# Expert weights: a longer way from load to split, other staging room, and scatters without an order among themselves

## The chip, the cores and the metric

The kernel runs on one core of a Trainium2 chip. The time is the device time of one execution in microseconds (us), less is better. The engines are TensorE (PE in the profile, with its weight loads as PEld), VectorE (DVE), ScalarE (ACT), GpSimd (POOL) and SyncE (SP), which here only issues DMA transfers. Each engine works through its own queue strictly in order; semaphores order the queues among each other.

## What is computed

Attention with global and local keys and a bias by distance feeds a dense layer with the activation h - tanh(h), and that feeds a layer of eight experts of which each token takes one. The reference, cut to its core:

```
x = attention(q, k, v)            # 3072 tokens x 512
h = x @ w_in                      # 512 x 2048, the dense layer
x = (h - np.tanh(h)) @ w_out
logits = x @ w_gate               # the layer of experts
e_idx = np.argmax(logits, axis=1)
gate_w = softmax(logits)[e_idx];  eom = sigmoid(x @ w_output_gate)
for e in range(8):
    mask = e_idx == e
    h = np.maximum(x[mask] @ w1[e], 0.0)          # 512 x 1024
    out[mask] = gate_w[mask] * eom[mask, e] * (h @ w2[e])
```

Every product is made of three matmuls in a reduced 32-bit float: each operand is split into a high part (a cast) and a low part (the operand minus its high part), and high x high, high x low and low x high are added up in PSUM.

## The kernel before

The 3072 tokens go through in 12 blocks of 256. A list of numbered sub-steps (`at(gt, rank, fn)`, 32 per block) says in which order the program is written; from that a scheduler, which works with a timeline of its own, makes the order of the instructions in each engine's queue. Position in the list is therefore a wish, and the queues are the fact.

The dense layer (`moe_h`, `moe_y`) takes 16 slices u of 128 columns of w_in in each block: 12 matmuls `ph`, on ACT and DVE the activation (`uu`, `tt`, `ss`, `vt`, `gg`), its high part `gh` on ACT and its low part `gl` (on DVE in block 0, on POOL in the others), and then 6 matmuls `y`: four with `gh`, two with `gl`.

After a block comes the routing: the rows of y go to `yrow` (`rt_evac`), are transposed (`yT`), the logits come out of `lp` and `lg`, the rank of each token within its expert out of `rk`, and from it DVE makes the row address `su`. Two scatters on POOL, 128 rows each, then write the rows to the sorted buffer `srt` in DRAM (`scatter`). `cnt_c` counts the tokens of each expert.

The experts work in jobs. Expert 0, the one with the most tokens, has two: job 0 takes its first 256 rows, which are known once block 10 has been scattered, and job 1 the other 256, which need block 11 as well. Jobs 2 to 8 are the experts 1 to 7. A job loads its rows (`xr`, on SP's queue), transposes them on PE (`xTp`), splits them (`xTh` on ACT, `xTl` on DVE), and then goes through 8 steps f: 12 matmuls `h2p`, the split with Relu (`h2h` on ACT, `h2l` on DVE), and 6 to 12 matmuls `ob`. At its end the results go to `orow` and are scattered to the output.

The weights of an expert come in eight pieces of 512 KB: 0 to 3 of w1 and 4 to 7 of w2. `ex_load` issues the load on SP into a staging tile `ex`, `ex_split` makes the high part `eh` on ACT and the low part `el` on DVE. All staging tiles are of the tag "row" of three buffers, which `yrow` and the `orow` of job 0 take as well. In the list, piece f of the next expert is loaded in step f of a job and piece f - 1 is split in it.

Of the kernel before, what the change touches and what calls it, by code (L numbers as in the profile page):

```python
# [9 lines left out]
F32 = mybir.dt.float32  # L10
# [22 lines left out]
def kernel(  # L33
# [15 lines left out]
    nc = tc.nc  # L49
    P = 128  # L50
# [3 lines left out]
    E, _, F = w1.shape  # L54
    TB = 256
    NBLK = NT // TB
# [13 lines left out]
    NF2 = F // P  # L70
# [9 lines left out]
    srt = dram.tile([E * RS, W], F32, name="srt")  # L80
# [3 lines left out]
    def w8(name, dt=F32R):  # L84
        t = persist.tile([P, 2048], dt, tag="w8", bufs=16, name=name)
        return t

    def rowt(name):
        t = persist.tile([P, 1024], F32, tag="row", bufs=3, name=name)
        return t  # L90

    def bank(tag, bufs, name):
        t = psum.tile([P, 512], F32, tag=tag, bufs=bufs, name=name)
        return t
# [35 lines left out]
    agenda = {}  # L130

    def at(gt, rank, fn):
        agenda.setdefault((gt, rank), []).append(fn)

    def run(gt):
        for rank in range(-2, 5):
            fns = agenda.setdefault((gt, rank), [])
            while fns:
                if rank == -2:
                    with tc.high_priority():  # L140
                        fns.pop(0)()
                else:
                    fns.pop(0)()
# [453 lines left out]
    def moe_h(blk, u, gt):  # L597
        fg, fo = divmod(u, 4)
        ph = bank("h", 2, f"ph{blk}_{u}")
        n = 0  # L600
        for kc in range(KC):
            o = kc * 512 + fo * P
            whi, wlo = wih[fg][:, o : o + P], wil[fg][:, o : o + P]
            for lw, xx in ((whi, xhi), (whi, xlo), (wlo, xhi)):
                nc.tensor.matmul(ph[:, 0:TB], lw, xx[blk][:, kc, :], start=(n == 0), stop=(n == 3 * KC - 1))  # L605
                n += 1

        def tmp(tag, bufs, dt=F32):
            t = p1.tile([P, TB], dt, tag=tag, bufs=bufs, name=f"{tag}{blk}_{u}")
            return t  # L610

        L = {}

        def gate():
            hps = ph[:, 0:TB]
            uu = L["uu"] = tmp("uu", 2)
            ss = L["ss"] = tmp("ss", 2)
            tt = L["tt"] = tmp("tt", 2)
            vv = L["vv"] = tmp("vt", 2)
            nc.scalar.activation(uu, hps, AF.Square)  # L620
            nc.scalar.activation(tt, hps, AF.Tanh)  # L621
            nc.scalar.activation(ss, uu, AF.Square, scale=G_S, bias=ga[:, 0:1])  # L622
            nc.vector.scalar_tensor_tensor(out=vv, in0=uu, scalar=G_C, in1=hps, op0=ALU.add, op1=ALU.mult)  # L623
            nc.vector.tensor_tensor(out=tt, in0=tt, in1=hps, op=ALU.subtract)  # L624
            nc.vector.scalar_tensor_tensor(out=vv, in0=ss, scalar=G_S2B, in1=vv, op0=ALU.add, op1=ALU.mult)

        def gate2():
            uu, ss, tt, vv = L["uu"], L["ss"], L["tt"], L["vv"]
            gg = L["gg"] = tmp("gg", 2)
            if blk < 1:  # L630
                nc.scalar.activation(ss, uu, AF.Relu, bias=nt2[:, 0:1])
            else:
                nc.vector.tensor_scalar(out=ss, in0=uu, scalar1=G_T2, scalar2=None, op0=ALU.is_gt)
            nc.vector.tensor_tensor(out=gg, in0=vv, in1=uu, op=ALU.mult)  # L634
            nc.vector.copy_predicated(gg, ss.bitcast(I32), tt)  # L635

        def parts():
            gg = L["gg"]
            gh = tmp("gh", 3, F32R)
            gl = tmp("gl", 3, F32R)  # L640
            nc.scalar.copy(gh, gg)  # L641
            by = nc.vector if blk < 1 else nc.gpsimd
            by.tensor_tensor(out=gl, in0=gg, in1=gh.bitcast(F32), op=ALU.subtract)  # L643
            g_t[blk, u] = (gh, gl)

        at(gt + 1, 0, gate)
        at(gt + 2, 0, gate2)
        at(gt + 3, 0, parts)

    def moe_y(blk, u):  # L650
# [14 lines left out]


    rts = {}
    last_rows = []

    def rt_evac(blk):  # L670
        for j in range(2):
# [24 lines left out]
    def rt_logits(blk, gt):  # L696
# [92 lines left out]
        def scatter(j):  # L789
            r = rts.pop((blk, "row", j))  # L790
            store = nc.gpsimd.indirect_dma_start(
                out=srt[:, :], out_offset=IndirectOffsetOnAxis(ap=L["su"][:, j : j + 1], axis=0),
                in_=r[:, 0:W], in_offset=None, bounds_check=E * RS - 1, oob_is_err=False,
            )
            if blk == NBLK - 1:
                last_rows.append(store.ins)
                if j == 1:
                    tc.declare_no_dep(last_rows[1], last_rows[0], reason="each token has one row")

        last = blk == NBLK - 1  # L800
        rk = -2 if last else 0
# [4 lines left out]
        at(gt + 3, rk, step4)  # L806
        at(gt + 3, rk, step5)
        at(gt + 4, rk, lambda: scatter(0))
        at(gt + (4 if last else 6), rk, lambda: scatter(1))

    def plan_route(blk, gt):
# [50 lines left out]
    def expert(r):  # L862

        if r not in ordering:
            ordering[r] = nc.values_load(
                order_i[0:1, r : r + 1], engines=[mybir.EngineType.SP], min_val=0, max_val=E - 1
            )
        return ordering[r]
# [4 lines left out]
    NP = 8  # L873

    def ex_load(e, i):
        st = rowt(f"ex{e}_{i}")
        rv = expert(e)
        if i < 4:
            nc.sync.dma_start(st, w1[ds(rv, 1), i * P : (i + 1) * P, :].rearrange("o p f -> p (o f)"))
        else:  # L880
            r = (i - 4) * 2 * P
            nc.sync.dma_start(
                st.rearrange("p (c d) -> p c d", c=2),
                w2[ds(rv, 1), r : r + 2 * P, :].rearrange("o (c p) d -> p (o c) d", p=P),
            )
        staged["e", e, i] = st

    def ex_split(e, i):
        hd, ld = (w1h, w1l) if i < 4 else (w2h, w2l)
        t = (i % 4) // 2  # L890
        if i % 2 == 0:
            hd[e, t] = w8(f"eh{e}_{i}")
            ld[e, t] = w8(f"el{e}_{i}")
        st = staged.pop(("e", e, i))
        sl = slice((i % 2) * 1024, (i % 2 + 1) * 1024)
        hi = hd[e, t][:, sl]
        nc.scalar.copy(hi, st)  # L897
        nc.vector.tensor_tensor(out=ld[e, t][:, sl], in0=st, in1=hi.bitcast(F32), op=ALU.subtract)  # L898
# [17 lines left out]
    def ex_rows(n):  # L916
        r, j0, _ = jobs[n]
        rv = expert(r)
        for j, m in tiles(n):
            t = job_tile(n, "xr", [P, W], F32, f"xr{n}_{j}")  # L920
            nc.sync.dma_start(t[0:m, :], srt[ds(rv * RS + (j0 + j) * P, m), :])
            xrows[n, j] = t
# [5 lines left out]
    def n_groups(n):  # L928
        return KC // 2 if jobs[n][2] == 256 else KC
# [238 lines left out]
    for blk in range(NBLK):  # L1168
        G = 32 * blk
        for u in range(NF):  # L1170
            g = G + 2 * u
# [7 lines left out]
    G = 32 * (NBLK - 1)  # L1179
    at(G - 32 + 20, 2, order_experts)  # L1180
    for i in range(NP):
        at(G + 10 + 2 * i, 0, lambda i=i: ex_load(0, i))
        at(G + 12 + 2 * i, 0, lambda i=i: ex_split(0, i))

    pools.update({
# [14 lines left out]
    for i in range(4):  # L1200
        at(G + 1 + 2 * steps[i], 4, lambda i=i: ex_load(1, i))
        at(G + 5 + 2 * steps[i], 4, lambda i=i: ex_split(1, i))
    for gt in range(min(g for g, _ in agenda), G - 32 + 24):
        run(gt)

    pa.release()
    p2a = ctx.enter_context(tc.tile_pool(name="p2a", bufs=1, side="right", reuse_waits="tile"))
    for k in range(3):
        pools["xr", k] = p2a, "xr", 4
    for nm in ("xTh", "xTl"):  # L1210
        pools[nm, 1] = p2a, "xTa", 4
    for gt in range(G - 32 + 24, 32 * NBLK + 32):
        run(gt)


# [32 lines left out]
    for n in range(1, len(jobs)):  # L1248
        e = jobs[n][0]
        for f in range(NF2):  # L1250
            ex_s1(n, f)
            if n == 1:
                for i in range(NP):
                    if steps[i] - NF2 == f:
                        ex_load(1, i)
                    if steps[i] + 2 - NF2 == f and i >= 4:
                        ex_split(1, i)
            elif e + 1 < E:
                ex_load(e + 1, f)
                if f >= 1:  # L1260
                    ex_split(e + 1, f - 1)
            if f >= 1:
                if n < len(jobs) - 1 or f - 1 < NF2 - LATE:
                    ex_s2(n, f - 1)
            elif n > 1:
                ex_s2(n - 1, NF2 - 1)
                ex_out(n - 1)
            if n + 1 < len(jobs):
                if f == 2:
                    ex_rows(n + 1)  # L1270
                if 4 <= f < 4 + n_groups(n + 1):
                    ex_T(n + 1, f - 4)
                if f == NF2 - 1 and n > 1:
                    ex_split(e + 1, NP - 1)

    n = len(jobs) - 1
    with tc.manual_schedule(engines={mybir.EngineType.PE}):
# [134 lines left out]
```

## Time and profile before

| what | value |
|---|---|
| median of 3 runs | 1174.91 us (1173.6 to 1175.56) |
| the profiled execution | 1180.22 us |
| its span in the trace | 1178.4 us |
| PE busy in the span | 1114.1 us, 95% |
| DVE, ACT, POOL busy | 854.4, 672.6, 215.1 us |

The profile is of one execution, 5.3 us above the median. A busy time counts an instruction from its start to its end; matmuls overlap each other, so their spacing is shorter than their duration (a matmul of 256 columns lasts 0.28 us and follows the one before it by 0.12 us).

### The profile page before, as it was taken

To read this page: it belongs to the slowest core of one execution; us is meant where nothing else is said; L and a number is where in the kernel's file an instruction comes from. 1 tells how busy PE (TensorE), PEld (TensorE's weight loads), DVE (VectorE), ACT (ScalarE), POOL (GpSimd) and SP (SyncE) were. 2 spreads that over 40 slices of the span, in tenths; PEclk is the share of its full clock that TensorE was granted. 3 is DMA by queue.
4 is the path that set the end of the run, shared out by engine and by line. 5 is a ranking of instruction groups with operands and counts; after the bars stand their busy time and mean duration, and the time that the engine had idled before them with its cause. 6 is when DMAs were issued, how large, how long until landed. Compare 5 with 4: busy or idle time off the path is not lost.

```text
span 1178.4 us, 22198 instructions
## 1 busy us (share of the span) xinstructions
PE 1114.1 (95%) x7374; PEld 948.8 (81%) x7374; DVE 854.4 (73%) x2704; ACT 672.6 (57%) x1794; POOL 215.1 (18%) x281
## 2 busy tenths in 40 slices
PE   3798899999999999999999999998999999999995
PEld 1476688888888888888888888887888778888894
DVE  4869978889989889989889888998463434434410
ACT  3989876666666666666666667565352333434310
POOL 1000012222222222222222222323100110110100
PEclk9799899999999999999999999999999999999998
DMA  6733492111211112121102121123471633625200
GB/s 177 237 105 122 143 275 53 28 48 33 55 38 39 37 39 51 30 55 30 49 21 55 37 55 26 38 72 110 136 260 59 204 97 107 206 91 163 78 23 24
DMA packets 128850, 103.25 MB, mean 88 GB/s; under 512 B 101679, under 2 KB 101679, under 8 KB 128720
## 3 DMA queue, kind: packets, MB, share of 16 engines
q1 hardware_dynamic: 124592, 89.06, 26.7%
q0 software_dynamic: 4128, 12.61, 2.8%
q8 instruction: 62, 1.02, 0.4%
q14 instruction: 68, 0.56, 0.2%
HBM read 90.04 MB, written 21.88 MB: 95 GB/s over the span
## 4 chain that ended last, share of the span: by engine, by line
PE 74%; DVE 7%; ACT 7%; DMA 5%; issue 5%; POOL 1%; SPq 1%; POOLq 0%; DVEq 0%; ACTq 0%
PE y L660 21%; PE ph L605 19%; PE ob L998 11%; PE h2p L971 9%; PE sc L495 3%; PE xp L558 3%; DMA ex<-in_moe_w_dram 3%; PE pt L544 2%; ACT pr L520 1%; PE wlo L268 1%; PE pk L431 1%; PE xTp L939 1%; PE yT L687 1%; DVE el L898 1%; DVE gg L634 1%
## 5 line engine op out<-in xcount | busy, mean ns | idle before, releaser
L643 POOL TENSOR_TENSOR gl<-gg,gh 128x256 fp32r<-128x256 f32 x176 | 148.3, 843 | 454.9 <-ACT gh L641 360.6
L605 PE MATMUL ph<-xhi,wh 128*128 128x256 f32 x768 | 219.1, 288 | 3.3 <-DVE tt L624 2.7
L605 PE MATMUL ph<-xhi,wl 128*128 128x256 f32 x768 | 218.6, 286 | 0.4 <-DVE wl L264 0.4
L605 PE MATMUL ph<-xlo,wh 128*128 128x256 f32 x768 | 217.2, 283 | 0.0
L660 PE MATMUL y<-wh,gh 128*128 128x512 f32 x384 | 158.7, 413 | 2.6 <-ACT gh L641 2.5
L605 PEld LDWEIGHTS ph<-xhi,wh 128*128 128x128 f32 x768 | 144.6, 189 | 16.6 <-DVE tt L624 5.3
L660 PE MATMUL y<-wl,gh 128*128 128x512 f32 x384 | 154.7, 403 | 0.0
L605 PEld LDWEIGHTS ph<-xlo,wh 128*128 128x128 f32 x768 | 145.0, 189 | 7.8 <-issue 0.3
L605 PEld LDWEIGHTS ph<-xhi,wl 128*128 128x128 f32 x768 | 144.8, 189 | 5.8 <-issue 3.7
L660 PE MATMUL y<-wh,gl 128*128 128x512 f32 x384 | 140.2, 411 | 2.5 <-POOL gl L643 2.5
L641 ACT CAST gh<-gg 128x256 fp32r<-128x256 f32 x192 | 78.8, 410 | 88.2 <-DVE gg L635 70.6
L976 DVE SCALAR_TENSOR_TENSOR h2l<-h2p,h2h 128x448 fp32r<-128x448 f32 (+3 forms) x72 | 40.0, 558 | 105.8 <-ACT h2h L975 105.8
L620 ACT ACTIVATE uu<-ph 128x256 f32<-128x256 f32 x192 | 74.0, 386 | 73.1 <-PE ph L605 65.8
L898 DVE TENSOR_TENSOR el<-ex,eh 128x1024 fp32r<-128x1024 f32 x64 | 77.7, 1223 | 50.2 <-ACT eh L897 49.4
L520 ACT ACTIVATE pr<-pr,sst 128x256 f32<-128x256 f32 (+1 forms) x192 | 93.5, 491 | 34.5 <-DVE sst L512 34.5
L623 DVE SCALAR_TENSOR_TENSOR vt<-uu,ph 128x256 f32<-128x256 f32 x192 | 79.9, 416 | 45.3 <-ACT tt L621 43.9
L975 ACT ACTIVATE h2h<-h2p 128x448 fp32r<-128x448 f32 (+3 forms) x72 | 35.4, 494 | 128.5 <-PE h2p L971 127.7
L897 ACT CAST eh<-ex 128x1024 fp32r<-128x1024 f32 x64 | 66.6, 1051 | 63.1 <-DMA ex<-in_moe_w_dram 48.0
L998 PE MATMUL ob<-eh,h2h 128*128 128x512 f32 x232 | 93.4, 403 | 7.4 <-ACT h2h L975 7.3
L622 ACT ACTIVATE ss<-uu,ga 128x256 f32<-128x256 f32 x192 | 99.5, 519 | 0.0
L971 PE MATMUL h2p<-xTh,eh 128*128 128x448 f32 (+3 forms) x288 | 98.0, 343 | 0.0
L971 PE MATMUL h2p<-xTl,eh 128*128 128x448 f32 (+3 forms) x288 | 97.6, 340 | 0.0
(199 smaller groups left out, 2521.7 us busy)
## 6 DMA issues: line engine op xcount, KB each, us to landing
ex<-in_moe_w_dram SPq DMA_DIRECT2D x64, 512.0 KB
vv<-vg SPq DMA_DIRECT2D x92, 96.0 KB
srt<-zrow SPq DMA_DIRECT2D x32, 257.0 KB
m<-in_moe_w_in_dram SPq DMA_DIRECT2D x16, 512.0 KB
m<-in_moe_w_out_dram SPq DMA_DIRECT2D x16, 512.0 KB
xr<-srt SPq DMA_DIRECT2D x25, 257.0 KB
qk<-in_q_dram SPq DMA_DIRECT2D x92, 64.0 KB
qk<-in_k_dram SPq DMA_DIRECT2D x92, 64.0 KB
```

The lines of the kernel that those rows point to most:

```text
L520: nc.scalar.activation(pr[j][:, c0:], pr[j][:, c0:], AF.Exp, bias=st[:, j : j + 1], scale=-1.0, accum_out=st[:, 2 + j : 3 + j],)
L605: nc.tensor.matmul(ph[:, 0:TB], lw, xx[blk][:, kc, :], start=(n == 0), stop=(n == 3 * KC - 1))
L620: nc.scalar.activation(uu, hps, AF.Square)
L622: nc.scalar.activation(ss, uu, AF.Square, scale=G_S, bias=ga[:, 0:1])
L623: nc.vector.scalar_tensor_tensor(out=vv, in0=uu, scalar=G_C, in1=hps, op0=ALU.add, op1=ALU.mult)
L641: nc.scalar.copy(gh, gg)
L643: by.tensor_tensor(out=gl, in0=gg, in1=gh.bitcast(F32), op=ALU.subtract)
L660: nc.tensor.matmul(yb[blk, j], gx[:, j * P : (j + 1) * P], wx[fg][:, sl], start=(u == 0 and n == 0), stop=(u == NF - 1 and n == 2),)
L897: nc.scalar.copy(hi, st)
L898: nc.vector.tensor_tensor(out=ld[e, t][:, sl], in0=st, in1=hi.bitcast(F32), op=ALU.subtract)
L971: nc.tensor.matmul(ph[:, 0:N], lw, xx, start=(i == 0), stop=(i == 3 * KC - 1))
L998: nc.tensor.matmul(ob[n, j][0:m, :], gx[:, j * P : j * P + m], wx, start=(f == 0 and i == 0), stop=(f == NF2 - 1 and i == 2),)
```

## The change

Four things are changed. Piece f - 2 instead of f - 1 is split in step f of a job, and the last two pieces in the first two steps of the next. The pieces of expert 0 and the first four of expert 1 are staged in tiles of the tag "xTa", four buffers, in which the odd jobs keep their transposed rows; for that the attention's room is given back 28 sub-steps earlier, and the loads of expert 0 are written 4 to 12 sub-steps earlier. The scatters to `srt` are declared free of each other in all blocks (before: only the two of the last block). And `gl` of the last block is made on DVE instead of POOL.

```diff
-            by = nc.vector if blk < 1 else nc.gpsimd
+            by = nc.vector if blk in (0, NBLK - 1) else nc.gpsimd
...
-            if blk == NBLK - 1:
-                last_rows.append(store.ins)
-                if j == 1:
-                    tc.declare_no_dep(last_rows[1], last_rows[0], reason="each token has one row")
+
+            tc.declare_no_dep(store.ins, group="srt", reason="each token has one row")
+            tc.add_to_no_dep_group("srt", store.ins)
...
     def ex_load(e, i):
-        st = rowt(f"ex{e}_{i}")
+        if e == 0 or (e == 1 and i < 4):
+
+            st = p2a.tile([P, 1024], F32, tag="xTa", bufs=4, name=f"ex{e}_{i}")
+        else:
+            st = rowt(f"ex{e}_{i}")
...
-        at(G + 10 + 2 * i, 0, lambda i=i: ex_load(0, i))
+        at(G + max(2 * i - 2, 2 * i + 4 if i >= 4 else 0), 0, lambda i=i: ex_load(0, i))
         at(G + 12 + 2 * i, 0, lambda i=i: ex_split(0, i))
...
-    for gt in range(min(g for g, _ in agenda), G - 32 + 24):
+    for gt in range(min(g for g, _ in agenda), G - 32 - 4):
...
-            elif e + 1 < E:
-                ex_load(e + 1, f)
-                if f >= 1:
-                    ex_split(e + 1, f - 1)
+            else:
+                if f < 2 and e > 1:
+                    ex_split(e, NP - 2 + f)
+                if e + 1 < E:
+                    ex_load(e + 1, f)
+                    if f >= 2:
+                        ex_split(e + 1, f - 2)
...
-                if f == NF2 - 1 and n > 1:
-                    ex_split(e + 1, NP - 1)
```

What this does to the queues is seen at three places. In the listings a name such as `h2p0_7` is that of job 0, step 7, `rk11` is of block 11, `ex1_4` is piece 4 of expert 1, and the last number only tells tiles apart; "..." marks rows left out.

PE, from the ranks of block 11 to the transposes of job 1, before:

```order
L761 MATMUL rk11_13491<-ohb11_13480,ones_bf_69 128x8
...
L971 MATMUL h2p0_5_13547<-xTh0_0_13239,eh0_0_12810 128x256
...
L830 MATMUL cnt_c_13649<-cnt_b_76,ones_bf_69 128x8
...
L971 MATMUL h2p0_7_13597<-xTh0_0_13239,eh0_0_12810 128x256
...
L998 MATMUL ob0_0_13395<-eh0_6_13131,h2h0_6_13587 128x512
...
L939 MATMUL xTp1_0_13673<-ident_66,xr1_0_13669 128x128
L939 MATMUL xTp1_1_13682<-ident_66,xr1_0_13669 128x128
...
L998 MATMUL ob0_0_13395<-eh0_6_13131,h2h0_7_13610 128x512
```

and now:

```order
L760 MATMUL rk11_13491<-ohb11_13480,ones_bf_69 128x8
L973 MATMUL h2p0_7_13597<-xTh0_0_13239,eh0_2_12931 128x256
...
L1000 MATMUL ob0_0_13395<-eh0_6_13133,h2h0_6_13587 128x512
...
L828 MATMUL cnt_c_13649<-cnt_b_76,ones_bf_69 128x8
L1000 MATMUL ob0_0_13395<-eh0_6_13133,h2h0_7_13610 128x512
...
L941 MATMUL xTp1_0_13673<-ident_66,xr1_0_13669 128x128
L941 MATMUL xTp1_1_13682<-ident_66,xr1_0_13669 128x128
```

The ranks have moved from step 4 of job 0 into the middle of `h2p0_7`: six `h2p` and twelve `ob` matmuls remain between them and the transposes, and the last six `ob` have moved ahead of these. Ahead of this place job 0's `h2p0_0` and `h2p0_1` begin before the last `y` products instead of after them.

ACT, at the start of job 1, before:

```order
L952 CAST xTh1_0_13678<-xTp1_0_13673 128x512
L952 CAST xTh1_0_13678<-xTp1_1_13682 128x512
L1011 ACTIVATE orow0_0_13634<-ob0_0_13395,so0_13270 128x512
L975 ACTIVATE h2h1_0_13708<-h2p1_0_13695 128x256
L897 CAST eh1_4_13756<-ex1_4_13712 128x1024
L975 ACTIVATE h2h1_1_13727<-h2p1_1_13714 128x256
```

and now:

```order
L1013 ACTIVATE orow0_0_13634<-ob0_0_13395,so0_13270 128x512
L954 CAST xTh1_0_13678<-xTp1_0_13673 128x512
L899 CAST eh1_4_13756<-ex1_4_13712 128x1024
L954 CAST xTh1_0_13678<-xTp1_1_13682 128x512
L899 CAST eh1_4_13756<-ex1_5_13760 128x1024
L977 ACTIVATE h2h1_0_13708<-h2p1_0_13695 128x256
L977 ACTIVATE h2h1_1_13727<-h2p1_1_13714 128x256
```

The cast of weight piece 4 has moved between the two casts of job 1's transposed rows, and that of piece 5 ahead of `h2h1_0`.

ACT, at the change from job 2 to job 3 (expert 1 to expert 2), as it now is; before, the same rows stand there in the same order:

```order
L977 ACTIVATE h2h2_7_14242<-h2p2_7_14229 128x480
...
L1013 ACTIVATE orow2_0_14324<-ob2_0_14009,so2_13935 128x512
L1013 ACTIVATE orow2_2_14334<-ob2_2_14011,so2_13935 128x512
L899 CAST eh3_2_14476<-ex3_3_14441 128x1024
L977 ACTIVATE h2h3_0_14292<-h2p3_0_14279 128x448
```

Nothing has moved here: the cast of piece 3 still stands ahead of `h2h3_0`.

## Rows read from the trace of the kernel before

**Rows 1.** The page, part 1: engine, busy us, share, instructions.
```profile
PE 1114.1 (95%) x7374; PEld 948.8 (81%) x7374; DVE 854.4 (73%) x2704; ACT 672.6 (57%) x1794; POOL 215.1 (18%) x281
```

**Rows 2.** Stages: from:to, length, busy us of PE, PEld, DVE, ACT, POOL, clock, DMA.
```profile
190.00:755.00 565.00, 560.78 (x4357) 495.79 (x4354) 506.46 (x1813) 368.01 (x1119) 146.30 (x186) 1.00 0.16 41
755.00:810.00 55.00, 54.10 (x366) 46.72 (x364) 51.57 (x147) 35.39 (x88) 18.50 (x19) 1.00 0.22 73
810.00:818.00 8.00, 5.97 (x17) 3.99 (x16) 5.89 (x10) 2.92 (x7) 5.12 (x6) 0.79 0.42 138
...
917.00:925.00 8.00, 6.21 (x30) 4.98 (x28) 2.32 (x7) 2.96 (x5) 3.87 (x4) 1.00 0.96 289
...
1053.00:1062.00 9.00, 6.75 (x39) 5.80 (x38) 3.57 (x7) 4.09 (x6) 3.84 (x4) 1.00 0.93 314
1062.00:1091.00 29.00, 29.00 (x139) 25.96 (x140) 13.91 (x21) 12.09 (x19) 0.00 (x0) 0.94 0.50 156
```

**Rows 3.** Waits of PE, 795 to 1178 us: total us, times, longest.
```profile
PE ob L998 <- ACT h2h L975: 7.3, 4, 2.2
PE y L660 <- POOL gl L643: 2.5, 2, 1.8
PE xTp L939 <- DMA xr<-srt: 1.2, 3, 0.6
```

**Rows 4.** The chain that ended last, 915 to 930 us: start, us, what.
```profile
914.99 0.12 PE xTp L939
...
917.30 6.10 DMA ex<-in_moe_w_dram
...
923.42 0.02 ACT eh L897
...
924.38 0.55 ACT h2h L975
```

**Rows 5.** Waits of POOL over the whole span: total us, times, longest.
```profile
POOL srt L791 <- DMA srt<-yrow,su: 24.0, 9, 3.2
```

**Rows 6.** Groups by line: PE in 812.5 to 817.4, then in 800 to 812 us.
```profile
L660 PE MATMUL y<-wl,gh 128*128 128x512 f32 x3 | 1.9, 628 | 0.0
L660 PE MATMUL y<-wh,gl 128*128 128x512 f32 x4 | 1.8, 538 | 1.8 <-POOL gl L643 1.8
...
L660 PE MATMUL y<-wl,gh 128*128 128x512 f32 x8 | 3.2, 395 | 0.0
```

**Rows 7.** gl and ss by line; DVE's ss in 755 to 830; timeline at 771.
```profile
L643 DVE TENSOR_TENSOR gl<-gg,gh x16: 405/422/427, 73.4 to 155.1; 128x256 fp32r<-128x256 f32 x16
...
L633 DVE TENSOR_SCALAR ss<-uu x176: 270/294/1266, 155.8 to 812.7; 128x256 f32<-128x256 f32 x176
...
L633 DVE TENSOR_SCALAR ss<-uu 128x256 f32<-128x256 f32 x19 | 8.8, 465 | 0.4
...
771.38 0.74 POOL L643 TENSOR_TENSOR gl<-gg,gh 128x256 fp32r<-128x256 f32 x1 [1.87 <-ACT gh L641]
771.48 0.80 DVE L633 TENSOR_SCALAR ss<-uu 128x256 f32<-128x256 f32 x1
```

**Rows 8.** Timeline of PE, 834 to 847 us: start, duration, instruction, wait before it.
```profile
834.61 0.18 PE L761 MATMUL rk<-ohb,ones_bf 128*128 128x8 bf16 x1
...
845.03 0.41 PE L939 MATMUL xTp<-ident,xr 128*128 128x128 f32 x2 [0.37 <-DMA xr<-srt]
845.63 0.87 PE L939 MATMUL xTp<-ident,xr 128*128 128x128 f32 x6 [0.19 <-DMA xr<-srt]
```

**Rows 9.** The chain that ended last, 834 to 850 us.
```profile
838.48 3.72 DMA srt<-yrow,su
...
842.76 2.83 DMA xr<-srt
...
846.51 1.41 PE ob L998 x6
847.91 2.15 PE h2p L971 x18
```

**Rows 10.** The page, part 5: the weight casts on ACT.
```profile
L897 ACT CAST eh<-ex 128x1024 fp32r<-128x1024 f32 x64 | 66.6, 1051 | 63.1 <-DMA ex<-in_moe_w_dram 48.0
```

More of the change, by code (lines that the diff above doesn't have):

```diff
@@ L667 @@
     rts = {}
-    last_rows = []
     def rt_evac(blk):
@@ L1211 @@
         pools[nm, 1] = p2a, "xTa", 4
-    for gt in range(G - 32 + 24, 32 * NBLK + 32):
+    for gt in range(G - 32 - 4, 32 * NBLK + 32):
         run(gt)
```

## Prediction

> **What bounds the kernel now.** The page comes first: of the span, TensorE (PE) is busy 95% [rows 1]. The end is therefore set by how many microseconds PE waits and by the stretches in which its clock is at the lower of its two levels (1.2 instead of 2.4 GHz). Next the table by stages, to see where PE is not full [rows 2]. In the 565 us of the middle blocks it is idle 4.2 us, so there is nothing to win there. The idle time sits in the passage from the dense layer to the experts (0.9 us in 755 to 810, 2.0 us in 810 to 818, where the mean clock falls to 0.79) and in short stretches at the changes of experts (1.8 us in 917 to 925, 2.25 us in 1053 to 1062, with 0.94 of the clock in the 29 us behind it). Third, who made PE wait after 795 us: ScalarE's `h2h` (7.3 us in four waits, all at changes of experts), GpSimd's `gl` (2.5 us in two, both in the last block) and the row loads `xr` (1.2 us in three) [rows 3]. Fourth, the chain at a change of experts [rows 4]: the row loads of the next job wait in SyncE's (SP's) queue for the transposes `xTp`, the weight piece stands behind them, needs 6.10 us, and ScalarE (ACT) waits for it in a cast `eh` with `h2h`, which PE needs, queued behind.
>
> **Part 1, the split two sub-steps after its load.** The stall to be removed is the cast of `ex3_3` ahead of `h2h3_0`. The queues, not the Python loop, decide this. From the row of `h2h2_6` on, ACT's queue is row for row that of before (the third listing), and so are VectorE's (DVE's), PE's and SP's from there. The four waits stay: **0**, where their full removal would be -7.3 us [rows 3] and some -1.7 us of slow clock (0.06 of 29 us [rows 2]), -9.0.
>
> **Part 2, the scatters.** In blocks 0 to 10 GpSimd (POOL) waited 24.0 us for the first scatter's landing, nine times [rows 5]. What stood behind it is `gl`, and PE waited for `gl` only in the last block, so nine blocks give **0** (at most the 4.2 us of idle time of the middle blocks, which have other releasers). The two scatters of block 11 were free of each other before. What changes is block 10: the second scatter no longer waits, and the first job's rows come earlier.
>
> **Part 3, the last dense block: `gl` to DVE, expert 0's weights early.** To win: the 2.5 us of waits for `gl`, and the slow clock behind the longer one, where 11 `y` matmuls took 538 to 628 ns in the mean of their group, instead of about 395 [rows 6], some 2 us: -4.5. To lose: DVE takes 16 `gl` of 422 ns [rows 7], 6.8 us, and in 755 to 810 it was busy 51.6 of 55 us [rows 2], so 3.4 are free. It gets part of that back: `ss`, one of its own operations, has a median of 294 ns but a mean of 465 over the 19 instructions of 755 to 830 us, 3.3 us in all, and a long one (0.80 us) stands right beside a `gl` on POOL [rows 7]. The Trainium skill says that DVE and GpSimd take one shared port pair of SBUF as an exclusive lock and that the later one blocks (SBUF — State Buffer, section "SBUF: two separate sides"); by that rule the move is nearly free and this part alone would be worth its whole -4.5 us. The trace agrees as far as 294 against 465 ns go. Against it stands the queue: the split pieces now come in clusters, four `el` in a row around `gg_6`, so `gl` and `gg` of the neighbouring steps run late and PE meets them after `ph_7`, `ph_10` and `ph_12`. And expert 1's first four pieces are no longer held by row room, so SP issues them right behind the first job's rows, and ACT has `eh1_0` ahead of `xTh0_0` and three more casts ahead of `gh_15`. These are 4 x 512 + 2 x 257 KB, 2.6 MB, 8.2 us at the highest rate in the table (314 GB/s [rows 2]), while PE has some 5 us of work left; an estimate of 2 to 4 us of waits. I take **0** between -4.5 and +5.
>
> **Part 4, the rows of job 1.** This is the term that decides. Job 1 takes rows that block 11 scatters. From the last `rk` (834.79) to the first `xTp` of job 1 (845.03) the chain took 10.2 us [rows 8]: the addresses `su` on DVE, POOL, the scatter's 3.72, SP, the row load's 2.83 [rows 9]. Before, PE had work all that time and waited only 0.37 + 0.19 us. The change starts job 0 ahead of the last `y` products, so `y_15`, the logits and `rk` of block 11 slide back through job 0 (first listing). Behind the last `rk` there now stand 6 matmuls of `h2p` and 12 of `ob` before `xTp1_0`: 6 x 0.119 + 2 x 1.41 [rows 9] = 3.5 us. Exposed: 10.2 - 3.5 = 6.7, less the 0.56 that was waited before: **+6.1**. One `h2l` less inside the DVE steps may shorten it by 0.6 (bounds 5.5 and 6.7). The Trainium skill gives a DMA about 2.0 us of fixed cost besides its bytes (DMA: Bandwidth & Descriptors, section "Anatomy of one DMA — SWDGE (gpsimd) path"). An estimate with 2.0 us for each of the two transfers makes the chain 7.7 us and the wait 3.6 instead of 6.1.
>
> **Part 5, the start of job 1.** (a) The last six `ob`, which stood behind the transposes and covered their casts, now stand ahead: PE waits for the first cast and subtraction, **+1.0** (0.5 to 1.4, the 1.41 us of cover). (b) In ACT's queue the cast `eh1_4` now stands between the two casts of job 1's transposed rows (second listing), and its piece is issued behind the late row loads. It may take 6.10 us [rows 4] where the rows take 2.83 [rows 9]: issued 0.6 us later, it lands up to 3.9 us after them, and the cast itself is 1.05 [rows 10]. Against that PE has 14 matmuls of 0.119, 1.7 us. The subtraction `el1_4` blocks DVE in the same way. **+2** (0 to 4).
>
> **Part 6, the clock.** After waits of about 2 us it fell in two places and not in a third [rows 2]: 0.21 of 8 us, 0.06 of 29 us, and 0. After 6 us of waiting I expect a fall: **+1.5** (0 to 3.4, two such falls).
>
> **The sum.** 0 + 0 + 0 + 6.1 + 1.0 + 2 + 1.5 = 10.6 us. The profiled execution took 1180.2 us (its span is 1178.4), so one of the changed kernel would take about 1190.8. The median of the timed runs is 1174.9, 5.3 us lower; with the same difference it goes to **1185.5 us**, 0.9% slower. With all low bounds it is +1.5 (1176.4), with all high ones +20.5 (1195.4).
>
> **Rivals.** *The waits at the changes of experts go.* For it: the loop now asks for one sub-step more between load and split. Against it: the unchanged rows in all queues. Price -9.0: 1176.5 with my other terms, and it makes the kernel faster as soon as these come to less than 6.7 us, which their low bounds allow. *The last block gains all it can*: part 3 at -4.5, hence 1181. For it the long `ss` beside `gl`; against it DVE's 51.6 of 55 us. (It is what the lock rule of the Trainium skill, SBUF — State Buffer, would bring.) *ACT's queue costs more than I think*: part 3 at +5, part 5 and the clock at their high ends, hence 1193 to 1195; for it that ACT, like PE, takes its queue strictly in order behind loads of up to 6.10 us. *The change does little*: every term comes out at its low bound, and 1176 to 1177 results; against it the 3.72 and 2.83 us of this very chain.
>
> **How the numbers follow.** Two measurements of this kernel differ by about 0.2%, 2.35 us, without a change. Forecast with the gain of the last block inside it, 1177.3 to 1193: 0.68, of which 0.13 belong to the gain of the last block. Above 1193: 0.07. Within 0.2%: 0.10, half of it the first rival with my other terms. Faster: 0.15, the first rival with low other terms, and what I have not seen. So slower 0.75, same 0.10, faster 0.15. The range reaches down into the cases of no change, 1175 to 1193; forecast alone 1177.3 to 1193.
>
> **What would show it.** Part 4: PE waits 5 to 7 us at `xTp` <- DMA `xr`, right after `cnt_c` and the last `ob` of job 0, and `rk` of block 11 comes only some 3.5 us of PE work ahead of it. Part 5: ACT waits for DMA `ex` in `eh` right after that, and PE for `xTh` or `xTl`. Part 1: still about 7 us in four waits `ob` <- `h2h`. Part 3: no `y` <- POOL `gl`, but waits `y` <- `gh`, and `ss` near 0.29 us in the last block. Part 6: a lower granted clock in the stage of job 1. The prediction is wrong if the wait at `xTp` is under 3 us, if the four waits at the changes of experts are gone, or if the last block wins more than 5 us.

## The result, and the profile after

The changed kernel takes 1182.5 us (median of 4 runs, 1181.83 to 1185.3), the kernel before 1174.26 in the same comparison (4 runs, 1172.44 to 1175.56). The ratio is 1.0072, 95% interval 1.0054 to 1.0089: 8.2 us between the medians, where 10.6 were forecast (1185.5). The profiled execution has a span of 1180.1 us. The first part of its page answers to [rows 1]:

```profile
PE 1110.6 (94%) x7374; PEld 945.4 (80%) x7374; DVE 848.5 (72%) x2720; ACT 670.6 (57%) x1794; POOL 198.3 (17%) x265
```

PE has the same number of instructions and almost the same busy time; the loss is idle time, and slow clock inside busy time. Who made PE wait from 755 to 1182 us (us in total, times, longest), beside [rows 3]:

```profile
PE xTp L941 <- DMA xr<-srt: 7.6, 5, 5.7
PE ob L1000 <- ACT h2h L977: 4.7, 3, 1.9
PE h2p L973 <- ACT xTh L954: 2.2, 2, 1.6
PE y L660 <- ACT gh L641: 2.1, 4, 0.8
PE ob L1000 <- ACT eh L899: 1.5, 1, 1.5
PE y L660 <- DVE gl L643: 0.3, 1, 0.3
```

The first row has grown from 1.2 us in three: one wait alone is 5.7 us, for the row loads. The waits for `gl` on POOL are gone, and those at the changes of experts (`h2h`, `eh`) are still there. PE's timeline at the long wait, from the last rank of block 11, beside [rows 8]:

```profile
840.62 0.17 PE L760 MATMUL rk<-ohb,ones_bf 128*128 128x8 bf16 x1
...
842.85 0.18 PE L828 MATMUL cnt_c<-cnt_b,ones_bf 128*128 128x8 bf16 x1
...
850.25 0.66 PE L941 MATMUL xTp<-ident,xr 128*128 128x128 f32 x2 [5.72 <-DMA xr<-srt]
851.36 1.54 PE L941 MATMUL xTp<-ident,xr 128*128 128x128 f32 x6 [0.45 <-DMA xr<-srt]
...
856.45 0.51 PE L973 MATMUL h2p<-xTh,eh 128*128 128x256 f32 x2 [0.60 <-ACT xTh L954]
857.37 0.44 PE L941 MATMUL xTp<-ident,xr 128*128 128x128 f32 x2 [0.41 <-DMA xr<-srt]
```

From the end of the last `rk` (840.79) to the first transpose 9.46 us pass, where before 10.2 passed [rows 8]. The chain did not grow; the PE work beside it shrank to 3.7 us. What PE was waiting for shows in the chain of work that ended last (start, us, what), beside [rows 9]:

```profile
841.46 0.18 DVE su L784
...
842.49 0.34 POOL srt L790
...
843.86 3.31 DMA srt<-yrow,su
...
848.57 6.27 DMA ex<-in_moe_w_dram
854.86 1.06 ACT eh L899
...
855.95 1.23 DVE el L900
857.17 0.20 DVE xTl L955
```

Behind the scatter (3.31 us) the chain goes on through weight piece 4, its cast and its subtraction, because these stand in ACT's and DVE's queues ahead of the second half of job 1's rows. The stages (as [rows 2]) show the clock behind the wait:

```profile
190.00:755.00 565.00, 560.80 (x4358) 495.93 (x4357) 502.55 (x1813) 368.46 (x1122) 144.33 (x185) 1.00 0.16 40
...
810.00:818.00 8.00, 5.24 (x27) 3.74 (x28) 6.28 (x19) 4.83 (x9) 0.00 (x0) 1.00 0.80 293
845.00:850.00 5.00, 0.00 (x0) 0.00 (x0) 0.75 (x1) 0.07 (x1) 1.95 (x2) 0.85 0.64 209
850.00:856.00 6.00, 5.11 (x20) 3.92 (x20) 1.18 (x6) 1.72 (x3) 0.00 (x0) 0.56 1.02 352
856.00:862.00 6.00, 5.12 (x34) 4.43 (x35) 4.47 (x14) 3.57 (x6) 0.00 (x0) 1.00 0.91 284
```

In the middle blocks nothing changed (560.80 us of 565 busy, before 560.78). In 810 to 818 us, the last dense block, the clock is full now (before 0.79), but PE is busy for less of it (5.24 us, before 5.97). After the wait the granted clock is 0.56 in the mean for 6 us, mostly the lower of its two levels, and then full again.

Profiled executions lie some us apart at the start and the end (block 10's first `yT` came between 765.3 and 771.2 us in the 14 profiles of this study, with no clear order by the parts). So I measure a **passage** inside each profile: from block 10's first `yT` on PE to the first `orow` of job 2 on ACT. Both ends in the changed kernel:

```profile
766.91 0.60 PE L686 MATMUL yT<-ident,yrow 128*128 128x128 f32 x4
...
926.25 0.69 ACT L1013 ACTIVATE orow<-ob,so 128x512 f32<-128x512 f32 x1 [2.19 <-PE ob L1000]
```

That is 159.3 us. In the second profile of the kernel before (last but one of the experiments) it is 148.7, in the first 148.9. The change costs 10.4 to 10.7 us there; from this `orow` to the first one of job 6 both kernels take the same, 176.9 and 177.05 (second profile of before).

### The profile page after: what moved, and what is told of

Its sections match the earlier page's. It is cut to its first block, busy times and chain, and to the rows that moved or that the text cites. A ratio compares the mean times of both kernels' runs of the same rounds, so it can differ in the third digit from the quotient of the medians.

```text
span 1180.1 us, 22184 instructions
## 1 busy us (share of the span) xinstructions
PE 1110.6 (94%) x7374; PEld 945.4 (80%) x7374; DVE 848.5 (72%) x2720; ACT 670.6 (57%) x1794; POOL 198.3 (17%) x265
## 4 chain that ended last, share of the span: by engine, by line
PE 78%; ACT 6%; DMA 5%; DVE 5%; issue 4%; SPq 1%; POOL 0%; POOLq 0%; ACTq 0%; DVEq 0%
PE y L660 21%; PE ph L605 20%; PE ob L1000 11%; PE h2p L973 10%; PE sc L495 4%; PE xp L558 4%; DMA ex<-in_moe_w_dram 3%; PE pt L544 3%; PE wlo L268 1%; PE pk L431 1%; DVE el L900 1%; ACT pr L520 1%; PE yT L686 1%; PE xTp L941 1%; PE pq L428 1%
## 5 line engine op out<-in xcount | busy, mean ns | idle before, releaser
L643 POOL TENSOR_TENSOR gl<-gg,gh 128x256 fp32r<-128x256 f32 x160 | 131.4, 821 | 450.9 <-ACT gh L641 347.7
L973 PE MATMUL h2p<-xTh,el 128*128 128x448 f32 (+3 forms) x288 | 97.6, 340 | 0.0
```

What stands on the lines that cost most here:

```text
L973: nc.tensor.matmul(ph[:, 0:N], lw, xx, start=(i == 0), stop=(i == 3 * KC - 1))
```

## The experiments

**Theory A:** the loss is the chain of block 11's rows, exposed by as much as PE lacks work behind the last `rk`, and the start of job 1 behind it. **Theory B:** the early weights or the busier DVE slow the last block by themselves. **Theory C:** the difference is one of single executions.

In this section edit 1 is the later split, edit 2 the free scatters, edit 3 `gl` on DVE, and edit 4 the staging tiles with the earlier loads. The Parts of the prediction are cut otherwise: its Part 3 holds edits 3 and 4, and its Part 4 is the wait that follows.

Edit 1 needed no run. Built alone on the kernel before, or taken out of the changed one, it leaves all five queues as they were, row for row: the list of sub-steps is written otherwise, and the scheduler makes the same program of it.

**The other edits, one at a time, and the change without edit 3.**

```diff
 p3_only, on the kernel before
-            by = nc.vector if blk < 1 else nc.gpsimd
+            by = nc.vector if blk in (0, NBLK - 1) else nc.gpsimd
 p4_only, on the kernel before
-        st = rowt(f"ex{e}_{i}")
+        if e == 0 or (e == 1 and i < 4):
+            st = p2a.tile([P, 1024], F32, tag="xTa", bufs=4, name=f"ex{e}_{i}")
+        else:
+            st = rowt(f"ex{e}_{i}")
...
-        at(G + 10 + 2 * i, 0, lambda i=i: ex_load(0, i))
+        at(G + max(2 * i - 2, 2 * i + 4 if i >= 4 else 0), 0, lambda i=i: ex_load(0, i))
...
-    for gt in range(min(g for g, _ in agenda), G - 32 + 24):
+    for gt in range(min(g for g, _ in agenda), G - 32 - 4):
 p2_only, on the kernel before
+            tc.declare_no_dep(store.ins, group="srt", reason="each token has one row")
+            tc.add_to_no_dep_group("srt", store.ins)
 no_p3, on the changed kernel
-            by = nc.vector if blk in (0, NBLK - 1) else nc.gpsimd
+            by = nc.vector if blk < 1 else nc.gpsimd
```

> The kernel before with only the gl of the last block on DVE. In the queues this alone puts job 0's first two h2p ahead of the last y, the last rk back, and leaves 11 ob (11 x 0.235 = 2.6 us) between the last rk and the first xTp of job 1. Theory A (the chain from rk over scatter and row load is exposed by as much as PE lacks work behind the last rk): PE waits 6.5 to 7.5 us at the first xTp <- DMA xr, the waits for gl go (-2.5), clock and start of job 1 cost 1 to 3 more, so slower by 5 to 9 us, 1179 to 1183. Theory B (the loss of the change comes from the weights being staged early, which fills ACT's queue and the DMA): this run is equal to before or 2 to 4 us faster, 1170 to 1174, no wait over 2 us at xTp. Theory C (the difference is that of single executions): within 2.4 us of before.

> The kernel before with only the staging of experts 0 and 1 in xTa tiles, their earlier loads and the earlier release of the attention's room. Between the last rk and the first xTp of job 1 there are 24 h2p and 18 ob (24 x 0.119 + 18 x 0.235 = 7.1 us). Theory A: PE waits 2 to 3.5 us at the first xTp, and the start of job 1 costs up to 1 more, so slower by 1.5 to 5 us, 1176 to 1179. Theory B: the whole loss, 7 to 9 us, 1181 to 1183. Theory C: within 2.4 us of before.

> The kernel before with only the scatters to srt free of each other in all blocks. Between the last rk and the first xTp of job 1 there are 22 h2p and 18 ob (22 x 0.119 + 18 x 0.235 = 6.8 us). Theory A: PE waits 2 to 3.5 us at the first xTp, and the start of job 1 costs up to 1 more, so slower by 1.5 to 5 us, 1176 to 1179; no gain in the blocks 1 to 9, where PE stays idle 4 us in 565. Theories B and C: within 2.4 us of before.

> The changed kernel with gl of the last block back on POOL; the other three parts stay. Between the last rk and the first xTp of job 1 there are the 36 h2p and 23 ob of before (36 x 0.119 + 23 x 0.235 = 9.7 us). Theory A: the wait at the first xTp is under 1 us, and the time is that of before, 1172 to 1177, with some 2 us of waits for gl. Theory B: the loss stays, 1180 to 1184. Theory C: within 2.4 us of before as well, but then p3_only is too.

**A slice more or less of `gl` on DVE, and the chain taken away.**

```diff
 mix8, on the changed kernel
-            by = nc.vector if blk in (0, NBLK - 1) else nc.gpsimd
+            by = nc.vector if blk < 1 or (blk == NBLK - 1 and u < 8) else nc.gpsimd
 no_chain, on the changed kernel (srt_b: 256 rows, filled once with zeros)
-            nc.sync.dma_start(t[0:m, :], srt[ds(rv * RS + (j0 + j) * P, m), :])
+            if n == 1:
+                nc.sync.dma_start(t[0:m, :], srt_b[j * P : j * P + m, :])
+            else:
+                nc.sync.dma_start(t[0:m, :], srt[ds(rv * RS + (j0 + j) * P, m), :])
```

> The changed kernel with gl on DVE in the first 8 of the last block's 16 slices, on POOL in the other 8. Between the last rk and the first xTp of job 1 there are 24 h2p and 21 ob (24 x 0.119 + 21 x 0.235 = 7.8 us). Theory A: the wait at xTp1 is about 9.5 - 7.8 = 1.7 us (1 to 2.5), the waits for gl and gh in the last block about 2, so 1174 to 1178, between before and p2_only. Theory B: half the loss of the change, 1177 to 1179, with the wait at xTp1 still near 5.

> The changed kernel, gl on DVE and all, but job 1 loads its 256 rows from a second buffer that is filled with zeros at the start (two loads more there); the real rows of job 1 are left out of the result. PE's queue is the same up to the last rk and behind the transposes of job 1, which now stand right behind cnt_c, and the cast of weight piece 4 of expert 1 no longer stands between the two casts of job 1's rows. Theory A (the loss is the wait for block 11's rows and what follows from it): no wait over 1 us at xTp1, no fall of the clock behind it, 1172 to 1176, the time of before. Theory B (gl on DVE slows the last block by itself, the wait only hides it): at most half of the 8 us comes back, 1178 to 1182.

Measured, in the order of the PE work that stands between the last `rk` and the first `xTp` of job 1 (the work as in the expectations; the time from `rk` to `xTp` and the wait from each profile's timeline of PE; each ratio is to the runs of the kernel before that were timed beside that kernel, whose median was 1174.26 for the change, 1173.55 for mix8 and no_chain, 1173.1 for the others):

| kernel | PE work behind `rk`, us | `rk` to `xTp`, us | first wait at `xTp`, us | passage, us | median, us | ratio to before (95%) |
|---|---|---|---|---|---|---|
| before (two profiles) | 9.7 | 10.2, 9.7 | 0.4, 0 | 148.9, 148.7 | 1173.1 | 1 |
| no_p3 | 9.7 | 9.7 | 0 | 150.5 | 1173.03 | 1.0005 (0.9987 to 1.0022) |
| mix8 | 7.8 | 9.1 | 1.15 | 150.2 | 1173.65 | 0.9992 (0.9976 to 1.0008) |
| p4_only | 7.1 | 8.7 | 1.47 | 154.1 | 1176.42 | 1.0016 (0.9998 to 1.0033) |
| p2_only | 6.8 | 10.0 | 3.02 | 152.9 | 1177.82 | 1.0037 (1.0019 to 1.0055) |
| the change | 3.5 | 9.5 | 5.72 | 159.3 | 1182.5 | 1.0072 (1.0054 to 1.0089) |
| p3_only | 2.6 | 9.5 | 6.70 | 163.3 | 1186.17 | 1.0092 (1.0068 to 1.0116) |
| no_chain | none needed | none | 0 | 148.6 | 1172.76 | 0.9986 (0.9969 to 1.0003) |

The transposes of the four other kernels as their timelines of PE have them, in this order: mix8, p4_only, p2_only, p3_only.

```profile
842.74 0.41 PE L941 MATMUL xTp<-ident,xr 128*128 128x128 f32 x2 [1.15 <-DMA xr<-srt]
```

```profile
845.99 0.41 PE L943 MATMUL xTp<-ident,xr 128*128 128x128 f32 x2 [1.47 <-DMA xr<-srt]
```

```profile
845.34 2.22 PE L938 MATMUL xTp<-ident,xr 128*128 128x128 f32 x8 [3.02 <-DMA xr<-srt]
```

```profile
853.17 0.66 PE L939 MATMUL xTp<-ident,xr 128*128 128x128 f32 x2 [6.70 <-DMA xr<-srt]
```

From `rk` to `xTp` it is 8.7 to 10.2 us in all seven kernels with the chain, whether 2.6 or 9.7 us of PE work stand in between (where the wait is 0, that work fills it, and the chain may be shorter), and the wait grows as the work shrinks. Theory A is what these runs show; C falls, and B falls with no_chain: with `gl` on DVE, the early weights and the late `rk` all in place, but no chain, the passage is that of before. As no_chain also takes the cast of weight piece 4 out from between job 1's casts, it shows the wait and the start of job 1 together, not each by itself. Three figures missed what was expected: p3_only is slower than 1179 to 1183, mix8 a little faster than 1174 to 1178, and the wait of p4_only is under 2 to 3.5. The edits don't add up (p2_only, p3_only and, not told from zero, p4_only cost 0.37, 0.92 and 0.16%, all together 0.72%), since each acts by the order that the scheduler makes: with edits 1, 2 and 4 together (no_p3) it puts the last `rk` back behind `h2p0_4`, and nothing is lost.

p3_only loses in a second place too. Its timeline of PE in the last block, and that of ACT there:

```profile
811.21 0.80 PE L660 MATMUL y<-wh,gh 128*128 128x512 f32 x1 [4.65 <-ACT gh L641]
...
809.80 1.04 ACT L897 CAST eh<-ex 128x1024 fp32r<-128x1024 f32 x1 [3.38 <-DMA ex<-in_moe_w_dram]
810.76 0.40 ACT L641 CAST gh<-gg 128x256 fp32r<-128x256 f32 x1
```

A weight cast that waits 3.38 us for its piece stands ahead of `gh`, and PE waits 4.65 us for that; from 810 to 820 us the granted clock is 0.50. The changed kernel, which loads the pieces earlier, has no wait for `gh` over 0.8 us, and a clock of 1.00 there. That edit 4 does this is likely and not shown, as no run has edits 3 and 4 alone. Nor is the cost all gone: in the changed kernel (ACT, ACT, PE) a weight cast waits 3.17 us ahead of `xTh` of job 0, and PE 1.61 us for that.

```profile
813.61 1.04 ACT L899 CAST eh<-ex 128x1024 fp32r<-128x1024 f32 x1 [3.17 <-DMA ex<-in_moe_w_dram]
814.56 1.07 ACT L954 CAST xTh<-xTp 128x512 fp32r<-128x512 f32 x2
...
815.19 0.51 PE L973 MATMUL h2p<-xTh,eh 128*128 128x256 f32 x2 [1.61 <-ACT xTh L954]
```

**The waits at the changes of experts.** Edit 1 was to remove them and doesn't reach them, so the other end was tried: the row loads that stand ahead of the weight pieces in SP's queue.

```diff
 rows_one_step_later, on no_p3
-                if f == 2:
+                if f == 3:
                     ex_rows(n + 1)
 rows_on_pool, on no_p3 (k = 2); rows_on_pool_late, on no_p3 (k = 4); mix8_rows_on_pool_late, on mix8 (k = 4); before_rows_on_pool_late, on the kernel before (k = 4)
-        rv = expert(r)
+        rv = expert(r) if n < k else expert(r, mybir.EngineType.Pool)
...
-            nc.sync.dma_start(t[0:m, :], srt[ds(rv * RS + (j0 + j) * P, m), :])
+            q = nc.sync if n < k else nc.gpsimd
+            q.dma_start(t[0:m, :], srt[ds(rv * RS + (j0 + j) * P, m), :])
```

> no_p3 with the row loads of the next job written in step 3 instead of step 2. In SP's queue they then stand behind piece 3 and ahead of piece 4, and ACT has the cast of piece 4 ahead of h2h of step 0. If the place in SP's queue is the cause: piece 3 comes in time, piece 4 is now the late one, the waits stay within 2 us of those of no_p3 and the time within 2.4 us, 1171 to 1175. If only piece 3 was critical: 3 to 6 us faster, 1167 to 1170.

Measured 1172.63 us, 0.9988 (0.9968 to 1.0009), and 5.2 us of waits in four behind 880 us. As the first alternative says: piece 4 is late now. Its chain at the change from job 2 to job 3:

```profile
916.29 6.01 DMA ex<-in_moe_w_dram
...
922.32 0.02 ACT eh L899
...
923.27 0.55 ACT h2h L977
```

> no_p3 with the row loads of jobs 2 to 8 issued on POOL's queue instead of SP's. The weight pieces no longer stand behind row loads that wait for transposes; the scheduler also puts the casts of pieces 3 and 4 earlier in ACT's queue, ahead of h2h of step 7. If the waits at the changes of experts come from the place of the row loads in SP's queue: the waits ob <- h2h after 900 us fall from some 5 to under 1.5 us in sum, the clock behind them stays up, 1164 to 1169. If they come from the casts being placed before their pieces can be there (staging room and 5.5 us of load): the wait moves one step forward, within 2.4 us of no_p3, 1171 to 1175.

Measured 1174.87 us, 0.9996 (0.9975 to 1.0017): the time of the second alternative, though the waits behind 880 us fell to 2.0 in two, near the first. The passage took 157.3 us, with a new wait of 2.6 us for `h2h` in job 1 (counted to job 2's last `ob` on PE, as its first `orow` now stands behind weight casts in ACT's queue, it is 156.3, in no_p3 152.6).

> no_p3 with the row loads of jobs 4 to 8 alone on POOL's queue; jobs 2 and 3 keep theirs on SP's, so that the queues up to h2h of job 2, step 6 are those of no_p3. In rows_on_pool the time from the first output scatter of job 2 to that of job 7 was 132.5 us against 134.2 in no_p3 and 136.1 before, and from there to that of job 8 37.8 against 39.9 and 43.7, but the passage before job 2's end was 5.5 us longer than in no_p3. If that loss comes from job 2's rows and the pieces that then run ahead of them: it is gone, and the gain at the changes of experts stays: 1168 to 1171. If the waits at the changes of experts only differ from one execution to the next: within 2.4 us of before, 1171 to 1176.

> The same with mix8 instead of no_p3 as the base. The two bases differed by 0.1% in their ratios to before, so the same is expected: 1168 to 1171 if the row loads' place in SP's queue costs the waits, 1171 to 1176 if not.

(The scatters that the first of these two counts as those of jobs 7 and 8 are those of jobs 5 and 6.) Measured 1167.74 us, 0.9959 (0.9941 to 0.9977), and 1169.56 us, 0.9955 (0.9937 to 0.9973). Both are faster than before. Waits of PE from 880 to 1150 us, in rows_on_pool_late:

```profile
PE ob L1001 <- ACT h2h L978: 0.5, 1, 0.5
```

SP's queue and POOL's in rows_on_pool_late at the change from job 2 to job 3:

```profile
909.59 2.64 SPq L884 DMA_DIRECT2D ex<-in_moe_w_dram  x3
915.16 26.84 SPq L881 DMA_DIRECT2D ex<-in_moe_w_dram  x4
...
911.94 0.60 POOL L924 DMA_DIRECT2D xr<-srt  x1 [33.84 <-PE xTp L942]
```

POOL waits 33.84 us for the transposes and has no other work in that time, while SP goes on with the pieces. From job 2's first `orow` to that of job 6 this kernel takes 167.2 us, no_p3 174.05. But nearly 3 of these 7 us come of the mark: two weight casts now stand ahead of that first `orow` in ACT's queue, where in no_p3 it goes as soon as `ob` is there. From job 2's last `ob` on PE to job 6's it is 167.0 against 171.0 us.

```profile
916.00 2.00 ACT L899 CAST eh<-ex 128x1024 fp32r<-128x1024 f32 x2 [2.12 <-PE ob L1001]
917.90 1.26 ACT L1014 ACTIVATE orow<-ob,so 128x512 f32<-128x512 f32 x2
```

> The kernel before, unchanged, for a second profiled execution. From block 10's first yT to the first output scatter of job 2 it took 149.9 us in the first one, which is the order of the queues and should be the same within 1 us; the four waits ob <- h2h at the changes of experts, 7.3 us in the first one, were 1.8 to 5.2 us in other kernels with the same rows in ACT's queue there, so 3 to 7 us are expected.

Measured: one run of 1174.31 us, a passage of 148.7, and these waits of PE from 755 to 1182 us:

```profile
PE ob L998 <- ACT h2h L975: 5.1, 5, 2.1
PE y L660 <- POOL gl L643: 2.5, 2, 1.8
PE ob L998 <- ACT eh L897: 1.3, 1, 1.3
PE xTp L939 <- DMA xr<-srt: 0.8, 2, 0.6
```

The passage repeats within 0.3 us. The waits at the changes of experts sum to 6.2 here (0.2 of the 5.1 are in job 1) and 7.3 in [rows 3], so they vary by about 1 us from one execution to the next; the first profile also lost 2.8 us more from job 2 to job 6 (179.9 against 177.05), some 1.7 of it in the slow clock of 1062 to 1091 us [rows 2].

> The kernel before with nothing but the row loads of jobs 4 to 8 on POOL's queue. From block 10's first yT to the first output scatter of job 2 it took 149.6 us in before_again and 152.4 in rows_on_pool_late; from there to the first of job 7 136.2 against 132.0, and on to that of job 8 40.9 against 36.3. If the two places add up (the passage of before, the changes of experts of rows_on_pool_late): 4.2 + 4.6 = 8.8 us less than before, 1163 to 1167, with under 1 us of waits after 880 us. If the gain at the changes of experts needs the change's other parts: 1168 to 1171, like rows_on_pool_late; if it is of single executions: within 2.4 us of before.

Measured 1166.89 us, 0.9951 (0.9935 to 0.9966): 5.7 us less than before, the least of the study. The time lies in the first alternative's range, but the gain is not the 8.8 of the sum, and the waits are not under 1 us. Its profiled execution still has 4.1 us of waits behind 880 us:

```profile
PE ob L999 <- ACT h2h L976: 4.1, 4, 1.3
```

So the place of the row loads in SP's queue costs time, since moving those of jobs 4 to 8 gained 0.4 to 0.5% on three bases. That the whole gain comes through these waits is not shown: against the profile of each base they are 2.4 us shorter in rows_on_pool_late, 0.9 in mix8_rows_on_pool_late (3.7 against 4.6) and 2.1 to 3.2 here, for gains of 4 to 6 us. Why the same rows in ACT's queue wait 0.5 us in one kernel and 4.1 in another stays open; the profile with 0.5 is of the fastest of that kernel's runs (1165.74 us), the one with 4.1 of the slowest (1170.15), so single executions may account for it.

## Why the prediction was right, and where its terms were off

- **Part 1, forecast 0: right.** The waits at the changes of experts are 4.7 + 1.5 us, in the second profile of before 5.1 + 1.3. The rival that they go falls; the queues are the same row for row.
- **Part 2, forecast 0: right in the blocks, wrong alone.** 560.80 of 565 us against 560.78. But alone (p2_only) it costs 0.37%, through the order of `rk` and not through the scatters. The prediction took the shift of `rk` as one fact of the whole change and did not see that single edits cause it. Edit 3 alone does the most (2.6 us of work left), edits 2 and 4 less.
- **Part 3, forecast 0 between -4.5 and +5: right.** The `gl` waits of 2.5 us became 2.1 + 0.3 for `gh` and `gl`, and job 0's first `h2p` waits 1.6 us for `xTh`, where 2 to 4 us were estimated for the early weight pieces. All waits of PE from 755 to 835 us grew from 3.5 to 5.3 us, and the 1.7 us of slow clock of [rows 2] (0.21 of 8 us) are gone: the 0 is a gain and a loss that cancel. DVE's `ss` fell from 465 ns in the mean to this, in 755 to 830 us:

```profile
L643 DVE TENSOR_TENSOR gl<-gg,gh 128x256 fp32r<-128x256 f32 x16 | 6.7, 419 | 1.2 <-ACT gh L641 1.2
L633 DVE TENSOR_SCALAR ss<-uu 128x256 f32<-128x256 f32 x19 | 6.4, 335 | 0.2
```

The traces thus bear out that `ss` is slowed beside POOL's `gl`: in the same window it is 417 to 493 ns in before, no_p3, p2_only and p4_only, with `gl` on POOL, and 311 to 336 in the changed kernel, p3_only, no_chain and mix8, with `gl` or half of it on DVE. 19 x 0.13 = 2.5 us come back. The Trainium skill's lock between DVE and GpSimd (SBUF — State Buffer, section "SBUF: two separate sides") agrees with that direction. The gain of 4.5 us that its rival gave did not come: in no_chain, where the chain is away and the rest stays, the passage is 148.6 against 148.7.
- **Part 4, forecast +6.1: right.** Measured 5.72 + 0.45, less the 0.56 of before [rows 8], +5.6. The 0.6 us less that the prediction allowed for the missing `h2l` show: from the last `rk` to the end of `su` it is 0.83 us, before 1.45. Seven kernels along one line show the mechanism. The wait of 3.6 us that came out of the Trainium skill's fixed cost (DMA: Bandwidth & Descriptors, section "Anatomy of one DMA — SWDGE (gpsimd) path") was too short, as from `rk` to `xTp` it is 8.7 to 10.2 us in every profile, not 7.7. That estimate left out the bytes: by the fit of the same section, which holds for transfers issued from GpSimd, 257 KB at 436 GB/s add 0.6 us to each, an estimate of 8.9 us for the chain and 4.8 for the wait.
- **Parts 5 and 6, forecast +3.0 and +1.5: their sum right, their shares not.** From the first `xTp` of job 1 to job 2's first `orow` the change takes 76.0 us and no_chain 73.2, though no_chain has six `ob` (1.41 us) more to do there: 4.2 us, for 4.5 forecast. The visible waits are only 0.60 + 0.41. The clock has more: the eight transposes took 0.66 + 1.54 us instead of 0.41 + 0.87 [rows 8], and nine `h2p` behind them 2.39 us (852.94 to 855.33) instead of 9 x 0.119 = 1.07; 2.2 us in all. About 1 us is in neither. Part 5 was over-sized, by the timeline because PE, at the lower clock, took long enough over the first half of the rows to hide most of the late second half; no run tests that. Part 6 was under-sized by 0.7, so that the sum fits so well is partly luck.
- **The time.** The passage cost 10.4 to 10.7 us, for 10.6 forecast; the timed difference is 8.2. In the profiles the rest lies outside the passage: the changed kernel is 1.1 us earlier at block 10's `yT` and 1.8 us shorter behind job 6's first `orow` than the second profile of before. In five of the six other kernels of the table too, the passage (against 148.7) says 1.3 to 3.8 us more than the ratio. The queues hold the same rows there, but for a few that change places in blocks 0 to 8. The end gives most of it. Behind the last scatter to the output, with no engine computing, 11.2 us pass in the second profile of before (span 1172.5 us; 11.4 in the first) and 9.3 in the changed kernel (span 1180.1):

```profile
1160.34 0.97 POOL L1016 DMA_INDIRECT out_dram<-orow,ix  x1 [1.03 <-ACT orow L1011]
...
1169.87 0.98 POOL L1018 DMA_INDIRECT out_dram<-orow,ix  x1 [1.03 <-ACT orow L1013]
```

It is 9.0 to 9.3 us in mix8, p4_only, p3_only and no_chain too, and 10.9 in no_p3 and p2_only. At the start the granted clock from 0 to 160 us is 0.91 and 0.93 in the two profiles of before and 0.94 in the changed kernel; single executions differ there. What shortens the end stays open; the forecast of 1185.5 was too high by 3.
- **The other rivals.** ACT's queue does cost PE some us, as in p3_only (4.65 us behind a weight cast); in the changed kernel it is 1.61 us, far from the +5 of that rival. "The change does little" falls.

## What to carry to other kernels

A chain through DRAM (scatter, then load) has a length of its own; what it costs is that length less the work which the busiest engine's queue holds behind its start, so count that work in the queue after each change, also after one that seems to touch another engine only. A split list that is written later changes nothing where a scheduler decides; look at whether the queues differ at all before costing an edit. Where transfers that wait for buffers stand ahead of transfers that are urgent in one issuing queue, an idle engine's queue for the patient ones was worth 0.4 to 0.5% here for jobs 4 to 8, and nothing when the loads of jobs 2 and 3 moved as well.

## What the runs showed of the hardware that was not expected

- Not every wait of PE is followed by slow clock. From 845 to 875 us the mean granted clock was 1.00 in p4_only, whose longest wait there was 1.47 us, 0.89 in p2_only (3.02 us), 0.89 in the changed kernel (5.72) and 0.83 in p3_only (6.70). The changed kernel was at 0.56 for six us, and full again after that although it still waited 0.6 and 0.4 us.
- The row loads issued from POOL's queue took 5.8 us in the median from issue to landing (21 loads of 257 KB in rows_on_pool); on SP's queue a single one took 2.83 [rows 9]. That is not like with like: the 5.8 count from the start of the issue and are a median over loads that run beside weight pieces, the 2.83 from the end of the issue; that POOL's queue is the slower one is not shown. In rows_on_pool_late, where only jobs 4 to 8 load that way, PE waited for none of them.
